# Reassociated linear attention with a critical-path scheduler, in a kernel of four interleaved layers

## The chip, the cores and the metric

The kernel runs on one core of one Trainium2 chip. The metric is the device time of one execution in microseconds (us). Engines are named as in the profile: PE (TensorE matmul), PEld (its weight loads), DVE (VectorE), ACT (ScalarE), POOL (GpSimd), SP (SyncE, which here only issues transfers). A difference is taken from the ratio to the kernel before in the same rounds.

## The reference

Two pairs of layers, each an attention layer A and a feed-forward layer B, on x of 2048 x 512, all residual, LayerNorm before each layer. Cut to what matters:

```python
def A(x, wqkv, wo):                       # x is the LayerNorm of the stream, 2048 x 512
    q, k, v = split_heads(x @ wqkv)       # 32 heads of 16
    phi = lambda t: jnp.where(t > 0, t + 1, jnp.exp(t)) + 1e-6
    pq, pk = phi(q), phi(k)
    kv  = einsum("bhsd,bhse->bhde", pk, v)
    z   = einsum("bhsd->bhd", pk)
    num = einsum("bhqd,bhde->bhqe", pq, kv)
    den = einsum("bhqd,bhd->bhq", pq, z)[..., None] + 1e-6
    return merge_heads(num / den) @ wo
def B(x, w1, w2):                         # 512 -> 1376 -> 512
    return maximum(x @ w1, 0) @ w2
```

kv and z are sums over all 2048 rows. Nothing of the second half of an attention layer can start before its last row has gone through the first half. I call that point the barrier, and what comes before it the first phase. The second attention layer's first phase is interleaved with the feed-forward layer before it; the first attention layer's is not, since nothing is there to interleave with.

## The kernel before

The kernel is a graph of operations. A list scheduler, run when the kernel is built, gives each engine a fixed order from a table of assumed durations; every engine then executes its list strictly in that order, waiting on semaphores. 128 rows are a tile, 4 tiles a chunk, 4 chunks the sequence. The parts that matter (cut):

```python
# first phase, tile i: k and v projection, phi(k) to SBUF, v to SBUF, then the sum over rows
mm_group([(ps[b],  Tb[i, c], wqkv[c, D:2*D]) for c in range(4)])      # 4 x 512 columns
phi_evac(b, pk_tile(i))            # 2 ACT passes over PSUM, DVE min/add (emscr), DVE max
mm_group([(ps[b2], Tb[i, c], wqkv[c, 2*D:3*D]) for c in range(4)])    # 4 x 512 columns
evac(vext[i], ps[b2])              # ACT or DVE; column 128 of each block of vext is 1
mm_group([(kv_region(j), pk_tile(i)[j], vext[i, j, 0:129]) for j in range(4)])  # kv and z
...
# second half, chunk t, tile i
mm_group([(den, pq[j, t][il], Zh[j]) for il in range(4) for j in range(4)])  # 16 x 8 columns
DVE: dene = den + 1e-6 ; rden = reciprocal(dene)                              # rows x heads
mm_group([(num[j], pq[j, t][il], KVbd[j]) for j in range(4)])         # 4 x 128 columns
DVE: xn[i] = num * rden            # then 4 PE transposes (or a transposing DMA) back to Tb
mm_group([(ps[b], Tb[i, c], wo[c]) for c in range(4)])                # 4 x 512 columns
resid(i)                           # DVE adds the residual; ACT squares it for LayerNorm
```

```python
def _list_schedule(ops, ...):      # before
    ...
    for e in ENGINES:              # look at the next WINDOW[e] operations in program order
        ...                        # take the one that can start first; ties go to program order
```

The full text is here:

## Time and profile before

The median was 308.69 us before the prediction, over three runs from 308.55 to 308.80 us.

| what | before | where it is read |
|---|---|---|
| PE busy share of the span | 96% | busy row of the page |
| chain of waits, PE share | 81% | page, part 4 |
| matmul step, 512 columns | 215.9 ns | timeline of PE |
| DVE, ACT busy in 28 us at the first barrier | 26.8, 21.3 us | windows view |

The two lines of the page, kernel before (busy us, share of the span, count of instructions; then the chain that ended last):

```profile
...
PE 295.0 (96%) x1729; PEld 147.5 (48%) x1755; DVE 174.7 (57%) x486; ACT 178.3 (58%) x359; POOL 18.8 (6%) x29
...
PE 81%; DVE 11%; ACT 4%; DMA 3%; issue 1%
...
```

PE is the engine that the time follows. A "busy" PE is not one at its peak, because the shown matmuls overlap, so I use steps from start to start. The timeline of PE, kernel before, over the dense stretch (start us, us, engine, line, operation, count):

```profile
...
87.97 9.66 PE L499 MATMUL ps<-Tb,w 128*128 128x512 bf16 x44
97.47 0.38 PE L499 MATMUL ps<-w,big 128*128 128x512 bf16 x1
```

44 matmuls start between 87.97 and 97.47 us, 215.9 ns each. The Trainium skill, "TensorE: Matmul & The Clock Gate", Part 1, gives 215.7 ns for a warm matmul of 512 columns (columns divided by 2.4 GHz plus 2.5 ns), and this trace agrees. With this step every matmul's cost can be summed, and what is left of a stretch is time that PE lost.

### The profile page before, as it was taken

Reading aid. Unit: us, or ns where it says so; the run is one execution under the profiler, and the core shown is the slowest. Engines: PE = TensorE matmul, PEld = TensorE weight load, DVE = VectorE, ACT = ScalarE, POOL = GpSimd, SP = SyncE. Lnnn points to the kernel's source line nnn. Section 1 sums busy time; section 2 is a strip of 40 time slices with the busy share of each in tenths; the row PEclk is TensorE's granted clock in tenths of the full one; section 3 lists DMA queues with packets and bytes.
Section 4 is the critical chain, followed back from the end, with each engine's and each line's share of the span. In section 5 each row is a group of like instructions: output and inputs, shape, how many; then the busy total and the mean of one; then the engine's idle time right before and its main releaser. Section 6 shows DMA issues by size and latency. Waiting matters only on the chain.

```text
span 307.2 us, 4498 instructions
## 1 busy us (share of the span) xinstructions
PE 295.0 (96%) x1729; PEld 147.5 (48%) x1755; DVE 174.7 (57%) x486; ACT 178.3 (58%) x359; POOL 18.8 (6%) x29
## 2 busy tenths in 40 slices
PE   8999999898999999999999999989889999999996
PEld 3455555565444444444544445556534444444444
DVE  5898867999830381384264556699994026030122
ACT  1897857777775385387673357767867605606100
POOL 3211000001200020010000110000111001000000
PEclk9999999999999999999999999999999999999999
DMA  7993400003550016030000033000266002302022
GB/s 229 358 329 70 69 2 0 2 0 67 109 102 0 0 29 109 1 67 3 0 1 2 9 60 68 2 0 2 41 115 121 2 0 68 68 2 68 0 68 70
DMA packets 41765, 17.79 MB, mean 58 GB/s; under 512 B 33584, under 2 KB 41232, under 8 KB 41744
## 3 DMA queue, kind: packets, MB, share of 16 engines
q1 hardware_dynamic: 41744, 17.50, 24.0%
q8 instruction: 14, 0.23, 0.3%
q14 instruction: 7, 0.06, 0.1%
HBM read 7.01 MB, written 2.10 MB: 30 GB/s over the span
## 4 chain that ended last, share of the span: by engine, by line
PE 81%; DVE 11%; ACT 4%; DMA 3%; issue 1%
PE ps L499 78%; DVE xn L612 5%; DMA Tb<-xn 3%; DVE xres L510 2%; PE ps L394 2%; ACT big L479 2%; ACT escr L481 2%; DVE rden L596 2%; DVE xn L444 1%; PE ps L465 1%; DVE big L485 1%; DVE dene L594 0%; DVE emscr L483 0%; ACT Tb L469 0%; DVE xin L652 0%
## 5 line engine op out<-in xcount | busy, mean ns | idle before, releaser
L499 PE MATMUL ps<-Tb,w 128*128 128x512 bf16 (+1 forms) x352 | 77.3, 379 | 1.9 <-DMA Tb<-xn 1.9
L499 PE MATMUL ps<-w,big 128*128 128x512 bf16 (+3 forms) x355 | 76.4, 373 | 0.4
L633 ACT ACTIVATE big<-ps 128x512 bf16<-128x512 f32 (+1 forms) x78 | 46.2, 595 | 29.2 <-PE ps L499 28.8
L499 PE MATMUL ps<-wqkv,Tb 128*128 128x512 bf16 x248 | 58.3, 379 | 1.1 <-ACT Tb L469 0.7
L499 PEld LDWEIGHTS ps<-Tb,w 128*128 128x128 bf16 (+1 forms) x352 | 35.0, 100 | 43.5 <-DMA Tb<-xn 2.9
L499 PEld LDWEIGHTS ps<-w,big 128*128 128x128 bf16 (+1 forms) x363 | 35.3, 97 | 40.6
L516 ACT ACTIVATE sqscr<-xres 128x512 bf16<-128x512 f32 x48 | 30.1, 630 | 41.8 <-DVE xres L510 40.8
L479 ACT ACTIVATE big<-ps 128x512 bf16<-128x512 f32 x64 | 39.2, 613 | 19.1 <-PE ps L499 19.0
L510 DVE SCALAR_TENSOR_TENSOR xres<-ps,xres 128x512 f32<-128x512 f32 x32 | 21.7, 686 | 38.6 <-PE ps L499 38.4
L481 ACT ACTIVATE escr<-ps 128x512 bf16<-128x512 f32 x64 | 39.3, 616 | 0.0
L507 DVE TENSOR_TENSOR xin<-ps,xres 128x512 bf16<-128x512 f32 x15 | 10.4, 692 | 48.8 <-PE ps L499 48.8
L499 PEld LDWEIGHTS ps<-wqkv,Tb 128*128 128x128 bf16 x256 | 24.2, 97 | 26.6 <-ACT Tb L469 0.9
L499 PE MATMUL ps<-wo,Tb 128*128 128x512 bf16 x118 | 28.1, 379 | 2.4 <-ACT Tb L469 1.9
L432 POOL TENSOR_TENSOR rstd<-veps,nhalf 128x4 f32<-128x4 f32 x15 | 15.6, 1041 | 236.6 <-DVE veps L430 218.8
L499 PE MATMUL ps<-Tb,wqkv 128*128 128x512 bf16 x128 | 29.2, 379 | 0.0
L485 DVE TENSOR_TENSOR big<-big,emscr 128x512 bf16<-128x512 bf16 x64 | 26.6, 419 | 1.3
L529 DVE CAST vext<-ps 128x512 bf16<-128x512 f32 x23 | 15.9, 691 | 18.5 <-PE ps L499 18.4
L469 ACT ACTIVATE Tb<-ps 128x512 bf16<-128x512 bf16 x29 | 16.3, 600 | 16.7 <-PE ps L465 16.6
L483 DVE TENSOR_SCALAR emscr<-escr 128x512 bf16<-128x512 bf16 x64 | 18.1, 285 | 5.3 <-ACT escr L481 5.1
L612 DVE TENSOR_TENSOR xn<-ps,rden 128x512 bf16<-128x512 f32 x32 | 20.2, 680 | 0.0
L499 PEld LDWEIGHTS ps<-wo,Tb 128*128 128x128 bf16 x128 | 11.9, 98 | 14.6 <-ACT Tb L469 1.7
L499 PEld LDWEIGHTS ps<-Tb,wqkv 128*128 128x128 bf16 x128 | 12.1, 97 | 12.8
(57 smaller groups left out, 190.0 us busy)
## 6 DMA issues: line engine op xcount, KB each, us to landing
wqkv<-in_A_wqkv_dram SPq DMA_DIRECT2D x3, 512.0 KB, 5.9
xin<-in_A_x_dram SPq DMA_DIRECT2D x3, 512.0 KB, 8.7
out_dram<-xin SPq DMA_DIRECT2D x3, 512.0 KB, 2.9
w<-in_B_w_dram SPq DMA_DIRECT2D x1, 1376.0 KB, 11.0
w<-in_B_w_dram SPq DMA_DIRECT2D x1, 1280.0 KB, 13.8
wo<-in_A_wo_dram SPq DMA_DIRECT2D x1, 512.0 KB, 8.8
xin<-in_A_x_dram SPq DMA_DIRECT2D x1, 384.0 KB, 3.2
Tb<-xn SPq DMA_TRANSPOSE x16, 4.3
```

Of the source, the lines that this page charges most:

```text
L432: g.add(POOL, lambda e: e.tensor_tensor(rstd[:, sl], veps[:, sl], nhalf[:, 0:4], ALU.pow), [("veps", t), ("nhalf",)], [("rstd", t)], C_POO ...
L469: g.add_flex([(ACT, lambda e: e.activation(dst, psb()[:, :], ACTF.Identity), C_ACT_PSUM), (DVE, lambda e: e.tensor_copy(dst, psb()[:, :]), ...
L479: g.add(ACT, lambda e: e.activation(dst_ap, psv[:, b, :], ACTF.Identity, bias=1.0 + 1e-6, scale=1.0), [("ps", b)], [dst_key], C_ACT_PSUM, ...
L481: g.add(ACT, lambda e: e.activation(escr[:, s, :], psv[:, b, :], ACTF.Exp), [("ps", b)], [("escr", s)], C_ACT_EXP, name=name + "_exp")
L483: g.add(DVE, lambda e: e.tensor_scalar(emscr[:, s, :], escr[:, s, :], 1.0, 1e-6, ALU.min, ALU.add), [("escr", s)], [("emscr", s)], C_DVE_B ...
L485: g.add(DVE, lambda e: e.tensor_tensor(dst_ap, dst_ap, emscr[:, s, :], ALU.max), [dst_key, ("emscr", s)], [dst_key], 340.0, name=name + "_ ...
L499: last = e.matmul(o, l, r, start=st, stop=sp, skip_group_check=skip)
L510: g.add(DVE, lambda e: e.scalar_tensor_tensor(xres[:, i, :], psv[:, b, :], 0.0, src, ALU.add, ALU.add, accum_out=s1[:, i:i + 1]), [("ps", ...
L516: g.add(ACT, lambda e: e.activation(sqscr[:, q, :], xres[:, i, :], ACTF.Square, accum_out=s2[:, i:i + 1]), [("xres", i)], [("sqscr", q), ( ...
L529: (DVE, lambda e: e.tensor_copy(vext[:, i, :, 0:128], psv[:, b2, :].rearrange("p (j f) -> p j f", f=128)), C_DVE_FLEX)],
L612: g.add(DVE, lambda e: e.tensor_tensor(xn[:, i, :].rearrange("p (h f) -> p h f", f=16), psv[:, b, :].rearrange("p (h f) -> p h f", f=16), ...
L633: g.add_flex([(ACT, lambda e, M=M, b=b, u=u: e.activation(unit_ap(u, M), psv[0:M, b, :], ACTF.Relu), C_ACT_PSUM), (DVE, lambda e, M=M, b=b ...
```

## The change

The intent was to give PE less work. Since v = x wv, the sum of pk by v over the rows is (sum of pk by x) times wv. So the v projection and its eviction go, and the sum G = x^T pk is accumulated instead in four PSUM banks. kv is multiplied into wo once (Wp), and q is scaled by 1/den in the transposed layout in which it is produced, so that the products num, their transposes and 1/den in row layout go. z is summed by POOL. 1/den is exp(-ln(den)) on ACT, because den is now spread over 128 partitions. The scheduler is replaced as well: among the operations that can start now, it takes the one with the longest path to the end. The diff, cut to its core:

```diff
+        if i == 0: POOL: zacc = pk_tile(0)
+        else:      POOL: zacc = zacc + pk_tile(i)            # 128 x 512, f32 + bf16
-        v projection, eviction to vext, kv accumulation 4 x 129 columns
+    def a_g_acc(i, GB):      # 4 x 512 columns into 4 PSUM banks
+        mm_group([(ps[GB[c]], xn[i, c], pk_tile(i)) for c in range(4)])
...
+    def a_z_final():         # zhi, zlo: zacc in two bf16 halves; 8 matmuls with ones; Zbd = mask * z
+    def a_kv():              # KVT = mask * (wv^T G), 16 x 128 columns
+    def a_wp():              # Wp[j] = KVT[j]^T wo[j], 4 x 512 columns, 4 evictions
...
     def a_den(t):
-        16 matmuls of 8 columns; dene; reciprocal
+        for j in range(4):
+            mm_group([(ps[b], Zbd[j], pq[j, t])])            # 1 x 512 columns
+            ACT: lden = Ln(ps[b] + 1e-6)
+            ACT: lden = Exp(-lden)
+            DVE: pq[j, t] = pq[j, t] * lden
-    def a_num(i): ...        # num, xn = num * rden, transposes
     def a_wo(i):
-        mm_group([(ps[b], Tb[i, c], wo[c]) for c in range(4)])
+        mm_group([(ps[b], pq[j, t][il], Wp[j]) for j in range(4)])
...
 def _list_schedule(ops, ...):
+    succ = _prioritise(ops)  # longest path from each operation to the end
-    # earliest start within a window of program order
+    st0 = min(c[0] for c in cands)
+    st, o = min((c for c in cands if c[0] <= st0 + SLACK[e]), key=lambda c: (-c[1].prio, c[1].idx))
```

The full diff also preloads a table of functions on ACT.

## The prediction

> **What bounds it now.** TensorE. The page's busy row gives PE 96%; the chain of waits is PE for 81% of the span. The timeline of PE shows 44 FFN matmuls of 512 columns starting over 87.97 to 97.47 us, 215.9 ns each (the Trainium skill, "TensorE: Matmul & The Clock Gate", Part 1, gives 215.7 warm; the trace agrees). Issue steps from the timeline: 216 ns (512 columns), about 57 (128), 26 (the 8-column den). Sum before: 1216 x 216 = 262.3; kv accumulation 128 x 58 = 7.5; num 7.2; transposes 7.2; den 3.3; warm-up 6.6: 294 us of the 307.2 us span. The remaining 13 us: start 1.2, first transpose eviction 0.9, tail 2.7, and the two attention barriers, 55.5-77.6 and 202.3-224.8, each 18.3 us of PE work in 22 us: 3.8 and 4.2 lost. The rest is dense.
>
> **What the change does to PE, per attention layer.** Removes v projection (64 x 216), kv accumulation, num, den, 48 transposes: 25.4 us. Adds the x-pk accumulation (64 x 216 = 13.8), transposed den (16 x 216 = 3.5), wo folding (0.9), kvT and z (24 small, 1.3): 19.5 us. Net -5.9 per layer, -11.8 in all. PE sum 282 us.
>
> **Other engines.** Per layer, ACT and DVE together lose 16 v evictions, 12 Tb evictions, 4 reciprocals (0.95), and 16 xn multiplies (replaced by u multiplies of about the same 0.6-0.7). ACT gains 16 Ln + 16 Exp of 0.5-0.6 us (as the exp evictions): 17 us, all after z is known. At the barrier ACT has late phi 7.9 + Ln/Exp 17 + squares 10 = 35 us against some 22-26 us of PE work: the last chunks' den is ACT-bound, but FFN matmuls of chunk 0 (9.5 us each of h and out) should cover them once its transpose DMA (4.3 us) lands. New chain at the barrier: G eviction, kvT, mask, wo folding, eviction, 6-7 us, and z sum to Zbd, Ln, Exp, u, 9-10 us before the first wo; late q (6.9 us), kvT and den fill part. I put the hole at 3 to 5 us per barrier, as now: O transposes leave the chain, ACT's Ln/Exp comes in.
>
> **Contention.** 16 POOL adds of 128x512 per layer, taken as 1.25 us (the change's own constant). The Trainium skill, "SBUF — State Buffer", "Who interferes with whom", says two-SBUF-input and 2-port DVE instructions block while POOL holds the shared ports. No trace here shows it yet. In layer 0's first phase (10-50 us; DVE busy 34 us in the windows view, about 26 without v casts) 19 us of POOL adds could stretch phi and delay G: I allow 2 us. G also holds 4 PSUM banks instead of 2: 0-1 us.
>
> **Sum.** 308.7 - 11.8 + 2 (contention, banks) - 1 to +1 (barriers, scheduler): 298; with credit for the scheduler 297 us, range 290.5 to 303.5. Chances: faster 0.84, within 2% 0.13, slower 0.03.
>
> **What would show each step.** Matmul count: 1256 of 512 columns, no vext or KVbd, 32 transposes. PE idle in the two barriers: 3-5 us each, released by ACT (Ln/Exp) or DVE u. ACT near full for 20 us after each barrier. POOL adds about 1.2 us; DVE phi max/emscr rise above 419/285 ns in layer 0.
>
> **What would make it wrong.** POOL adds slower than 1.25 us, or DVE blocked so z or phi lags several us (303+). ACT not covered by FFN work, holes of 7-10 us. Barriers filled (289-291).

## More of the kernel before

The windows view, kernel before, of 28 us at the first barrier and 22 us at the second (each engine's busy us and count, PEclk, DMA share, GB/s):

```profile
...
50.00:78.00 28.00, 24.96 (x253) 15.25 (x254) 26.80 (x76) 21.27 (x49) 1.94 (x2) 1.00 0.11 20
203.00:225.00 22.00, 18.50 (x204) 11.87 (x205) 21.96 (x59) 14.72 (x35) 2.01 (x2) 1.00 0.18 26
...
```

Here PE has work for most of the time, but DVE is busy for 26.80 of 28 us and 21.96 of 22 us: at the barriers DVE, not PE, is full.

The start of DVE's list, kernel before (in brackets: idle time before the instruction and what ended it):

```profile
...
2.89 0.69 DVE L412 BATCH_NORM_STATS2 bst<-xin 128x6 f32<-128x512 bf16 x1 [1.71 <-DMA xin<-in_A_x_dram]
...
6.32 0.14 DVE L696 SCALAR_TENSOR_TENSOR nbias<-mv,rstd 128x1 f32<-128x1 f32 x1
...
6.54 0.38 DVE L698 TENSOR_SCALAR xn<-xin,rstd,nbias 128x512 bf16<-128x512 bf16 x1
...
```

The statistics of the first tile begin at 2.89 us, its nbias follows at 6.32 and its normalisation at 6.54 us. PE's first real work, a transpose, starts at 7.67 us, right behind its warm-up matmuls.

The DVE instructions that will meet POOL, kernel before, groups view of 8 to 60 us (x count, busy us, mean ns of one, idle us before them):

```profile
...
L485 DVE TENSOR_TENSOR big<-big,emscr 128x512 bf16<-128x512 bf16 x32 | 13.2, 416 | 0.5
...
L483 DVE TENSOR_SCALAR emscr<-escr 128x512 bf16<-128x512 bf16 x32 | 8.9, 282 | 0.9 <-ACT escr L481 0.7
...
L444 DVE TENSOR_SCALAR xn<-xin,rstd,nbias 128x512 bf16<-128x512 bf16 x13 | 4.6, 405 | 0.1
...
```

## The result, and the profile after

The changed kernel takes 319.45 us (median of four runs, 318.89 to 320.67), the kernel before 308.62 us: slower, ratio 1.0359 (95% interval 1.0338 to 1.0380). Here and below a ratio is one kernel's to the other's in the same rounds, so it is not quite the ratio of the medians. Differences "by ratio" below are differences of such ratios times 308.6 us.

The page's two lines, kernel after:

```profile
...
PE 290.7 (91%) x1363; PEld 131.2 (41%) x1363; DVE 185.1 (58%) x461; ACT 192.9 (61%) x388; POOL 58.9 (19%) x60
...
PE 69%; ACT 14%; DVE 9%; DMA 5%; issue 2%; SPq 0%; DVEq 0%
...
```

PE's share fell to 91%, and ACT and DVE entered the chain. I summed the matmuls of each stage at columns / 2.4 GHz + 2.5 ns, but at no less than 26 ns, the step of the 8-column matmuls in the timeline of before, and took the rest as lost. The trace of after has all 1363 matmuls; that of before lacks 26 of 1755 (5.6 us). Its 1755 weight loads are all there, so the stage of each missing matmul is known. The figures here, and those of the same kind below, are corrected for it:

| us lost by PE (span less matmul work) | before | after |
|---|---|---|
| first phase, to the last accumulating matmul | 5.3 | 16.6 |
| first barrier, to the first FFN matmul | 3.8 | 8.1 |
| FFN with the second first phase | 0.3 | 1.4 |
| second barrier | 4.2 | 8.4 |
| rest | 2.9 | 4.3 |
| all | 16.5 | 38.8 |
| matmul work | 290.7 | 279.0 |

The work fell by 11.7 us, as intended. The lost time rose by 22.3 us, and the difference is the 10.6 us that the span grew. The timeline of PE, kernel after, rows with a hole ahead of them:

```profile
...
1.24 4.93 PE L402 MATMUL ps<-wrm 128*128 128x512 bf16 x16 [1.24 <-DVE wrm L395]
11.39 1.77 PE L470 MATMUL ps<-ident,xn 128*128 128x128 bf16 x12 [5.21 <-ACT xn L697]
12.95 5.05 PE L504 MATMUL ps<-wqkv,Tb 128*128 128x512 bf16 x12
...
46.00 2.76 PE L504 MATMUL ps<-wqkv,Tb 128*128 128x512 bf16 x12 [3.09 <-DMA Tb<-xn]
...
81.43 3.59 PE L504 MATMUL ps<-Wp,big 128*128 128x512 bf16 x8 [4.72 <-DVE big L609]
...
233.22 5.86 PE L504 MATMUL ps<-Tb,w 128*128 128x512 bf16 x20 [3.48 <-DMA Tb<-xn]
...
```

There are three kinds of hole. PE waits 5.21 us at the start, and the 12 matmuls from 12.95 us then take 4.88 us, about 407 ns each instead of 216: the clock had gone down (PEclk 0.66 of full speed in the mean from 10 to 20 us). The same page of the skill says that an idle window of about 3.4 us halves the clock; the trace agrees here, and again after the 4.72 us hole, where 8 matmuls take from 81.43 to 84.82 us, 424 ns each. So 1.7 of the 8.1 us of the first barrier are slow matmuls and not waiting. After the 3.48 us hole the next 20 matmuls take 285 ns each, which puts 1.4 us more under "rest"; after the 3.09 us hole the clock is full (217 ns each). In the first phase PE waits 3.09 us for a transposing DMA. At the barriers it waits for DVE's multiply (L609) and for a DMA.

The start of DVE's list, kernel after, to be read against that of before:

```profile
...
6.83 0.17 DVE L704 TENSOR_SCALAR veps<-mv 128x3 f32<-128x3 f32 x1
9.14 1.29 DVE L417 BATCH_NORM_STATS2 bst<-xin 128x6 f32<-128x512 bf16 x2 [2.14 <-DMA xin<-in_A_x_dram]
10.34 0.14 DVE L693 SCALAR_TENSOR_TENSOR nbias<-mv,rstd 128x1 f32<-128x1 f32 x1
10.40 0.69 DVE L417 BATCH_NORM_STATS2 bst<-xin 128x6 f32<-128x512 bf16 x1
...
```

and POOL's at the same time:

```profile
...
6.79 0.58 POOL L691 TENSOR_TENSOR rstd<-veps,nhalf 128x1 f32<-128x1 f32 x1 [4.54 <-DVE mv L418]
...
```

The first tile's 1/std was ready on POOL at about 7.4 us. The nbias that needs it comes at 10.34 us, because two statistics of the second chunk (L417 at 9.14 us) stand ahead of it in DVE's list, and these waited for their load until 9.14 us. An engine takes its list strictly in order, so a load that lands later than the scheduler assumed holds back work that was ready.

The DVE groups of 8 to 60 us, kernel after, and the POOL adds:

```profile
...
L532 POOL TENSOR_TENSOR zacc<-zacc,big 128x512 f32<-128x512 f32 x15 | 20.5, 1370 | 14.8 <-DVE big L490 10.3 <-DVE veps L425 3.7 <-DVE nbias L439 0.6
...
L486 ACT ACTIVATE escr<-ps 128x512 bf16<-128x512 f32 x26 | 16.2, 631 | 11.9 <-PE ps L504 6.0 <-DVE emscr L488 5.9
...
L490 DVE TENSOR_TENSOR big<-big,emscr 128x512 bf16<-128x512 bf16 x25 | 13.9, 573 | 1.0 <-ACT big L484 0.5
...
L488 DVE TENSOR_SCALAR emscr<-escr 128x512 bf16<-128x512 bf16 x26 | 9.4, 380 | 1.3 <-ACT escr L486 1.0
...
L449 DVE TENSOR_SCALAR xn<-xin,rstd,nbias 128x512 bf16<-128x512 bf16 x13 | 7.5, 610 | 0.0
...
```

The mean of the phi maximum rose from 416 to 573 ns, emscr from 282 to 380, the normalisation from 405 to 610. Single instructions show why. DVE and POOL, kernel after:

```profile
...
22.22 1.36 DVE L449 TENSOR_SCALAR xn<-xin,rstd,nbias 128x512 bf16<-128x512 bf16 x1
```

```profile
...
22.27 1.15 POOL L532 TENSOR_TENSOR zacc<-zacc,big 128x512 f32<-128x512 f32 x1
...
33.38 3.70 POOL L532 TENSOR_TENSOR zacc<-zacc,big 128x512 f32<-128x512 f32 x1 [3.73 <-DVE veps L425]
37.04 1.01 POOL L437 TENSOR_TENSOR rstd<-veps,nhalf 128x4 f32<-128x4 f32 x1
```

The normalisation at 22.22 us took 1.36 us instead of 0.40 and ended when the POOL add of 22.27 us had ended. At 33.38 us it is the other way round: an add took 3.70 us beside an unbroken row of DVE instructions, phi maxima and emscr in turn, that ended at 36.06 us, and LayerNorm's power (L437), behind it in POOL's list, started only at 37.04 us.

The windows view of the barriers, kernel after:

```profile
...
56.00:85.00 29.00, 23.76 (x116) 9.92 (x115) 25.30 (x66) 28.20 (x60) 2.58 (x2) 0.90 0.10 19
203.00:233.00 30.00, 22.82 (x119) 10.12 (x115) 25.37 (x72) 29.77 (x67) 2.80 (x3) 0.99 0.15 19
...
```

ACT is busy for 28.20 of 29 us and 29.77 of 30 us; DVE is at 25.3 in both. ACT took on the load, and DVE was hardly relieved.

### The profile page after: what moved, and what is told of

Read it like the earlier page. It is cut to its first block, busy times and chain, and to the rows that moved or that the text cites. A ratio compares the mean times of both kernels' runs of the same rounds, so it can differ in the third digit from the quotient of the medians.

```text
span 317.8 us, 3874 instructions
## 1 busy us (share of the span) xinstructions
PE 290.7 (91%) x1363; PEld 131.2 (41%) x1363; DVE 185.1 (58%) x461; ACT 192.9 (61%) x388; POOL 58.9 (19%) x60
## 4 chain that ended last, share of the span: by engine, by line
PE 69%; ACT 14%; DVE 9%; DMA 5%; issue 2%; SPq 0%; DVEq 0%
PE ps L504 68%; ACT lden L607 3%; ACT lden L605 3%; DMA Tb<-xn 3%; DVE xn L449 3%; ACT sqscr L521 3%; ACT escr L486 2%; DMA xin<-in_A_x_dram 2%; ACT big L484 2%; DVE big L490 2%; DVE bst L417 2%; DVE emscr L488 1%; ACT xn L447 1%; PE ps L470 0%; DVE nbias L439 0%
## 5 line engine op out<-in xcount | busy, mean ns | idle before, releaser
L504 PE MATMUL ps<-w,big 128*128 128x512 bf16 (+2 forms) x363 | 77.3, 372 | 0.0
L486 ACT ACTIVATE escr<-ps 128x512 bf16<-128x512 f32 x64 | 38.8, 627 | 18.5 <-PE ps L504 10.1
L532 POOL TENSOR_TENSOR zacc<-zacc,big 128x512 f32<-128x512 f32 x30 | 38.5, 1283 | 35.9 <-DVE big L490 31.3
L437 POOL TENSOR_TENSOR rstd<-veps,nhalf 128x4 f32<-128x4 f32 x15 | 16.1, 1078 | 150.9 <-DVE veps L435 146.2
L504 PE MATMUL ps<-Wp,big 128*128 128x512 bf16 x128 | 31.4, 395 | 8.0 <-DVE big L609 6.6
L504 PE MATMUL ps<-wqkv,Tb 128*128 128x512 bf16 x128 | 33.3, 401 | 5.1 <-DMA Tb<-xn 3.1
L490 DVE TENSOR_TENSOR big<-big,emscr 128x512 bf16<-128x512 bf16 x64 | 34.7, 560 | 3.2 <-ACT big L484 2.1
L504 PE MATMUL ps<-big,xn 128*128 128x512 bf16 x128 | 30.1, 379 | 0.0
L488 DVE TENSOR_SCALAR emscr<-escr 128x512 bf16<-128x512 bf16 x64 | 21.4, 346 | 14.7 <-ACT escr L486 13.4
L504 PEld LDWEIGHTS ps<-Wp,big 128*128 128x128 bf16 x128 | 12.4, 100 | 25.3 <-DVE big L609 7.8
L504 PEld LDWEIGHTS ps<-wqkv,Tb 128*128 128x128 bf16 x128 | 12.7, 103 | 22.2 <-DMA Tb<-xn 3.6
L609 DVE TENSOR_TENSOR big<-big,lden 128x512 bf16<-128x512 bf16 x32 | 20.7, 685 | 1.3 <-ACT lden L607 1.2
L605 ACT ACTIVATE lden<-ps,eps 128x512 f32<-128x512 f32 x32 | 20.2, 718 | 1.1 <-PE ps L504 1.1
```

Source lines behind the costliest of these rows:

```text
L437: g.add(POOL, lambda e: e.tensor_tensor(rstd[:, sl], veps[:, sl], nhalf[:, 0:4], ALU.pow), [("veps", t), ("nhalf",)], [("rstd", t)], C_POO ...
L486: g.add(ACT, lambda e: e.activation(escr[:, s, :], psv[:, b, :], ACTF.Exp), [("ps", b)], [("escr", s)], C_ACT_EXP, name=name + "_exp")
L488: g.add(DVE, lambda e: e.tensor_scalar(emscr[:, s, :], escr[:, s, :], 1.0, 1e-6, ALU.min, ALU.add), [("escr", s)], [("emscr", s)], C_DVE_B ...
L490: g.add(DVE, lambda e: e.tensor_tensor(dst_ap, dst_ap, emscr[:, s, :], ALU.max), [dst_key, ("emscr", s)], [dst_key], 340.0, name=name + "_ ...
L504: last = e.matmul(o, l, r, start=st, stop=sp, skip_group_check=skip)
L532: g.add(POOL, lambda e: e.tensor_tensor(zacc[:, :], zacc[:, :], pk_tile(i), ALU.add), [("big", pk_unit(i)), ("zacc",)], [("zacc",)], C_POO ...
```

## The experiments

Two theories at the start. Theory M: the new arithmetic costs it, by POOL adds that block DVE and by Ln and Exp on ACT at the barrier. Theory S: the new scheduler's order costs it.

| run | us, median | ratio to before (95%) | output |
|---|---|---|---|
| after | 319.45 | 1.0359 (1.0338 to 1.0380) | |
| e1 new arithmetic, old scheduler | 320.07 | 1.0362 (1.0317 to 1.0406) | correct |
| e2 old arithmetic, new scheduler | 328.22 | 1.0637 (1.0577 to 1.0696) | correct |
| e3 after, loads in program order | 314.11 | 1.0196 (1.0159 to 1.0233) | correct |
| e4 after, POOL adds on 8 columns | 312.41 | 1.0137 (1.0100 to 1.0174) | wrong |
| e5 after, Exp on 8 columns | 317.29 | 1.0276 (1.0255 to 1.0298) | wrong |
| e6 e3, e4 and e5 together | 306.27 | 0.9924 (0.9876 to 0.9973) | wrong |
| e7 e3 and z on PE | 310.14 | 1.0060 (1.0032 to 1.0089) | correct |
| e8 e2, loads in program order | 315.35 | 1.0212 (1.0190 to 1.0235) | correct |
| e9 e7, Exp and u on 8 columns | 301.42 | 0.9753 (0.9707 to 0.9799) | wrong |
| e10 e7, 1/den in bf16 | 307.02 | 0.9943 (0.9911 to 0.9975) | correct |
| e11 e7, den on 32 partitions | 310.97 | 1.0048 (0.9992 to 1.0104) | correct |
| e12 after, POOL memsets for the adds | 318.27 | 1.0302 (1.0278 to 1.0325) | wrong |

The "8 columns" runs and e12 keep the scheduler's table of durations, so the order of the instructions is exactly that of their base kernel; the traces show the same order on all engines. Only the length of the named instructions differs, and in e12 their kind. A stage figure is of the one profiled execution of a kernel, a ratio of all.

### e1: the new arithmetic under the old scheduler

```diff
-def _prioritise(ops): ... ; def _list_schedule(...): ...   # new
+def _list_schedule(...): ...                               # that of before
```

> The new arithmetic, put in order by the old scheduler (its window, its strict choice of engine). Theory S (the new scheduler's static order is what costs the time: loads out of order at the start, DVE held behind a late load, POOL adds ahead of the LayerNorm power): most of the loss goes, 295 to 303 us. Theory M (the new arithmetic itself costs it: POOL adds that block DVE, Ln and Exp on ACT at the barrier): 312 us or more, whatever the order.

Measured: 320.07 us. Theory M holds for the arithmetic: with the old scheduler it is just as slow. The loss only sits elsewhere. PE starts at 7.30 us and the first phase loses 9.6 us instead of 16.6, but the barriers lose 8.8 and 10.8 us instead of 8.1 and 8.4, and the stretch between them 4.6 instead of 1.4.

### e2: the old arithmetic under the new scheduler

```diff
-def _list_schedule(...): ...                               # that of before
+def _prioritise(ops): ... ; def _list_schedule(...): ...   # new
```

> The old arithmetic, put in order by the new scheduler. Theory S: slower than the kernel before, 313 to 320 us, and the first layer's start is late as in the changed kernel. Theory M: 304 to 310 us.

Measured: 328.22 us, which is more than theory S gave. So both theories hold, each for its half, and the parts do not simply add up: the scheduler costs the old arithmetic 20 us by ratio and the new arithmetic nothing. The timeline of PE, e2, shows where most of it is:

```profile
...
21.63 1.89 PE L469 MATMUL ps<-ident,xn 128*128 128x128 bf16 x16 [14.54 <-DVE xn L448]
...
```

PE stands for 14.54 us at the start. The transfers of this run, SP's timeline, show the reason: the 128 KB first tile of x (L365), from which everything starts, was put behind four transfers of x and two of w, at 9.07 us instead of 0.80.

```profile
...
2.92 6.10 SPq L363 DMA_DIRECT2D xin<-in_A_x_dram  x2
9.07 1.93 SPq L365 DMA_DIRECT2D xin<-in_A_x_dram  x1
...
```

### e3: the loads in program order

```diff
-st, o = min((c for c in cands if c[0] <= lim), key=lambda c: (-c[1].prio, c[1].idx))
+st, o = min((c for c in cands if c[0] <= lim), key=lambda c: (-c[1].prio if e != SP else 0.0, c[1].idx))
```

> The changed kernel, but the SyncE queue takes its ready transfers in program order (first x tile, rest of its chunk, wk, ...), all else by priority. Wrongly ordered loads as a cause: first transpose back from 11.4 to about 7.7 us, no cold clock at 10 to 20 us, about 5 to 6 us less, 313 to 315 us. Rival: the first phase is bound by DVE and POOL after the start anyway, so the gain is absorbed before the barrier: 317 us or more.

Measured: 314.11 us, 5.0 us less than after by ratio. PE, e3, at the start:

```profile
...
7.00 0.40 PE L470 MATMUL ps<-ident,xn 128*128 128x128 bf16 x4 [0.77 <-DVE xn L695]
8.09 1.04 PE L504 MATMUL ps<-wqkv,Tb 128*128 128x512 bf16 x4 [0.69 <-ACT Tb L474]
...
```

The first transpose is at 7.00 us, PEclk is at full speed from 10 to 20 us. The order of the loads, and DVE's list that was planned on it, cost 5 us of the changed kernel. (The edit puts all of SP's transfers in program order, the transposing ones too.) Beside e1 it shows something else: with the loads in order, the new scheduler is about 5 us better for the new arithmetic than the old one (1.0196 against 1.0362). Its order of the compute gave what its order of the loads took.

### e4: short POOL adds

```diff
-tensor_tensor(zacc[:, :],   zacc[:, :],   pk_tile(i),         ALU.add)
+tensor_tensor(zacc[:, 0:8], zacc[:, 0:8], pk_tile(i)[:, 0:8], ALU.add)
```

> The changed kernel with the same order of instructions on each engine, but each POOL add works on 8 of 512 columns (wrong result on purpose)[...]. Contention as a cause: the DVE phi maximum falls from 560 to about 420 ns, the 3.1 us hole before 46 us goes, 312 to 315 us. Rival, the adds run beside DVE at no cost: within 1 us of 319.

Measured: 312.41 us, 6.9 us less by ratio. The groups of 8 to 60 us, e4:

```profile
...
L490 DVE TENSOR_TENSOR big<-big,emscr 128x512 bf16<-128x512 bf16 x26 | 10.5, 420 | 1.5 <-ACT big L484 1.4
...
L488 DVE TENSOR_SCALAR emscr<-escr 128x512 bf16<-128x512 bf16 x27 | 7.6, 290 | 6.3 <-ACT escr L486 6.0
...
L532 POOL TENSOR_TENSOR zacc<-zacc,big 128x8 f32<-128x8 f32 x15 | 5.3, 356 | 21.6 <-DVE big L490 15.4 <-DVE veps L425 5.2 <-DVE nbias L439 0.7
...
L449 DVE TENSOR_SCALAR xn<-xin,rstd,nbias 128x512 bf16<-128x512 bf16 x13 | 4.7, 404 | 0.0
...
```

DVE's three kinds of instruction are back at 420, 290 and 404 ns; together they took 22.8 us against 30.8 in the changed kernel. The hole before 46 us is gone. In the traces the whole gain lies in the first phase, which loses 9.9 us instead of 16.6, while the barriers stay at 8.1 and 8.5. The order on all engines is the same, so the length of the POOL adds is what differs. Not all of the gain need be theirs, though. PE in e4, the same 12 matmuls that took from 12.95 to 17.83 us in the changed kernel:

```profile
...
13.16 3.44 PE L504 MATMUL ps<-wqkv,Tb 128*128 128x512 bf16 x12
16.45 0.39 PE L470 MATMUL ps<-ident,xn 128*128 128x128 bf16 x4
...
```

They took 3.29 us instead of 4.88, before any POOL add had run: the clock came back earlier in this execution, by chance as far as the record shows. So the adds cost between 5.3 us (an estimate, 6.9 less 1.6) and 6.9 us.

### e12: POOL as long busy, but writing only

```diff
-tensor_tensor(zacc[:, :], zacc[:, :], pk_tile(i), ALU.add)
+memset(zscr[:, :], 0.0)                                # 128 x 1300 f32
```

> The changed kernel, same order of instructions, each POOL add replaced by a POOL memset of 1300 f32 columns, an estimated 1.1 to 1.2 us from the 128x128 memsets (wrong result on purpose): POOL is as long busy, but reads nothing from SBUF. If the 7 us of the adds are POOL's queue (LayerNorm's power behind an add): 317 to 320 us. If they are the shared read ports: two-input DVE instructions no longer wait (phi maximum mean back to about 420 ns) and the time falls to 312 to 315 us; one-input DVE instructions may still be stretched.

Measured: 318.27 us, only 1.8 us less by ratio. The groups, e12:

```profile
...
L532 POOL MEMSET zscr<- 128x1300 f32 x15 | 17.9, 1197 | 15.9 <-DVE big L490 15.0 <-DVE nbias L439 0.6
...
L486 ACT ACTIVATE escr<-ps 128x512 bf16<-128x512 f32 x26 | 15.8, 610 | 10.3 <-DVE emscr L488 5.2 <-PE ps L504 5.0
...
L488 DVE TENSOR_SCALAR emscr<-escr 128x512 bf16<-128x512 bf16 x26 | 15.3, 605 | 2.0 <-ACT escr L486 1.8
...
L490 DVE TENSOR_TENSOR big<-big,emscr 128x512 bf16<-128x512 bf16 x26 | 10.4, 417 | 1.0 <-ACT big L484 0.4
...
L449 DVE TENSOR_SCALAR xn<-xin,rstd,nbias 128x512 bf16<-128x512 bf16 x13 | 7.5, 617 | 0.0
...
```

Neither of my two readings was right as it stood. The two-input phi maximum does run freely again at 417 ns, as the reading by ports said, but the one-input emscr went to 605 ns and the normalisation stayed at 617, so DVE's three kinds take 33.2 us, no less than before. The Trainium skill, "SBUF — State Buffer", "Who interferes with whom", says just this: a DVE instruction with two SBUF inputs contends only with a POOL instruction that reads SBUF, a one-input instruction in a two-port mode with any. The trace agrees on both halves (that emscr and the normalisation run in such a mode, it does not show). What counts is that POOL is long busy at all while DVE runs such instructions. The queue can play only a small part: without the 3.70 us add, LayerNorm's power starts at 33.68 instead of 37.04 us and the hole before the DMA is 1.34 instead of 3.09 us. POOL and PE, e12:

```profile
...
33.68 1.04 POOL L437 TENSOR_TENSOR rstd<-veps,nhalf 128x4 f32<-128x4 f32 x1
...
44.06 2.76 PE L504 MATMUL ps<-wqkv,Tb 128*128 128x512 bf16 x12 [1.34 <-DMA Tb<-xn]
...
```

### e5: short Exp

```diff
-activation(lden[:, s, :],   lden[:, s, :],   ACTF.Exp, scale=-1.0)
+activation(lden[:, s, 0:8], lden[:, s, 0:8], ACTF.Exp, scale=-1.0)
```

> The changed kernel with the same order of instructions on each engine, but each Exp behind the Ln works on 8 of 512 columns (wrong result on purpose). The full Exp takes about 0.52 us of ACT per piece, the short one an estimated 0.2, so about 5 us of ACT less at each barrier. ACT's Ln and Exp as the cause of the barrier holes: the 4.7 us hole and the 1.3 + 1.9 + 3.5 us ones shrink to about half or less, 311 to 314 us. Rival, the holes come from the length of the chain G, kvT, wo folding and the transposing DMA: 317 us or more.

Measured: 317.29 us, 2.6 us less by ratio; the short Exp took 224 ns in the mean instead of 678. This spoke for the rival, that the holes are the latency of the chain. e9 corrected that: DVE was busy for 18.8 of the 20 us from 60 to 80 us in this run, so it could take over as the limit.

### e6: the three together

> Loads in program order, POOL adds on 8 columns and Exp on 8 columns together (wrong result on purpose). If the three costs stand side by side, they add up: 319.5 - 5.3 - 7.1 - (what the short Exp gave), so 300 to 302 us. If the first two give back the same slack of the first phase: 304 to 308 us.

Edit: those of e3, e4 and e5. Measured: 306.27 us. By ratio the three take away 13.4 us, against 5.0 + 6.9 + 2.6 = 14.5 us one by one. That is in the range that I had given to the rival, that the first two give back the same slack, and the traces bear it out in part: in the first phase e3 saves 6.3 us, e4 6.7, and the two together 9.1 (16.6 to 7.5). So the costs of the loads and of the adds overlap; over the whole kernel the difference of 1.1 us is within the noise (1.5 us).

### e7: ordered loads and z on PE, a correct kernel

```diff
-POOL: zacc = zacc + pk_tile(i) ; zhi, zlo, 8 matmuls with ones
+mm_group([(ps[zb][:, j], pk_tile(i)[j], ones[:, 0:1]) for i in range(16) for j in range(4)])  # end of phase
```

> A correct version of the first two: loads in program order, and z summed by 64 one-column matmuls into one PSUM bank at the end of the first phase (about 26 ns each as the 8-column den before, 1.7 us of PE per layer, and the eight zb matmuls go) in place of the POOL adds. If the POOL adds were the cost by their hold on the ports: 319.5 - 5.3 - 7.1 + 2 = about 309, 306 to 311 us. If the order of DVE work around them was the cost: 312 us or more.

Measured: 310.14 us, inside the expected 306 to 311. By ratio it is 9.2 us better than after; e3 and e4 gave 11.9, but they overlap (e6), and the 64 small matmuls per layer cost some of it. The kernel is now within 1% of the one before, though PE has about 9 us less to do. What remains is the barriers: 6.8 and 7.5 us lost in the profiled execution, the fastest of five (307.46 us).

### e8: the old arithmetic, new scheduler, ordered loads

> The old arithmetic with the new scheduler, but loads in program order. If the 20 us that the new scheduler cost the old arithmetic are its load order (PE idle 14.5 us at the start, then half clock): 309 to 313 us. If its choice of order elsewhere costs as much: 318 us or more.

Edit: that of e3, on e2. Measured: 315.35 us, between the two. By ratio, 13.1 us of the 19.7 us that the new scheduler cost the old arithmetic were the loads. The cause of the other 6.5 us stays open: the first phase, the first barrier and the end lose 2.0, 2.3 and 1.5 us more than in the kernel before, and I did not take them apart.

### e9: Exp and the multiply both short

```diff
 # e7 and
-tensor_tensor(pq, pq, lden, ALU.mult)
+tensor_tensor(pq[:, 0:8], pq[:, 0:8], lden[:, 0:8], ALU.mult)     # and Exp as in e5
```

> The version with ordered loads and z on PE, with Exp and the multiply u both on 8 of 512 columns (wrong result on purpose); same order of instructions. Short Exp alone had given 2 us. If the barrier is bound by ACT and DVE together (ACT 100%, DVE 84 to 97% busy there), taking about 5 us of ACT and 8 us of DVE per barrier closes most of the holes: 299 to 303 us against 310. If the holes are the latency of the chain and of the transposing DMA: 306 us or more.

Measured: 301.42 us, 9.5 us below e7 by ratio. The barriers lose 2.6 and 3.6 us instead of 6.8 and 7.5. PE at the longest hole of the first barrier, e7 and then e9:

```profile
...
71.80 4.11 PE L501 MATMUL ps<-Wp,big 128*128 128x512 bf16 x12 [3.71 <-DVE big L600]
...
```

```profile
...
69.39 2.76 PE L501 MATMUL ps<-Wp,big 128*128 128x512 bf16 x12 [1.75 <-DVE big L600]
...
```

The shorter hole also leaves the clock alone: the 12 matmuls behind it take 2.73 us instead of 3.95. The chain has the same number of links and the same DMA in both. One pass through it is shorter by an estimated 1.0 us (the means of Exp and multiply fell from 702 and 685 to 231 and 161 ns), against about 4 us less lost at each barrier, so its latency was not the main cause: at the barrier ACT and DVE together have too much to do, and relieving ACT alone (e5) gave only 2.6 us.

### e10: 1/den in bf16, a correct kernel

```diff
-ACT: lden = Exp(-lden)            # f32
+ACT: rdb  = Exp(-lden)            # bf16
-DVE: pq = pq * lden
+DVE: pq = pq * rdb
```

> The version with ordered loads and z on PE, but Exp writes 1/den in bf16, so that the multiply u has two bf16 operands (0.42 us as the phi maximum takes, not 0.69). About 4 us of DVE less per barrier, ACT as before. If DVE shares the bound: 305 to 308 us. If ACT alone binds the barrier: 309 to 311 us.

Measured: 307.02 us, correct. By ratio 3.6 us below e7 and 0.6% below the kernel before (interval 0.9911 to 0.9975): the only correct kernel here that beats both, by little. The barriers lose 5.4 and 6.1 us. That fits DVE sharing the bound, but the edit also lowered the multiply's duration in the scheduler's table, and the traces show another order on ACT and DVE than in e7, so the gain is not shown to be the multiply's alone.

### e11: den on 32 partitions

```diff
-for j: den[128 x 512] ; Ln ; Exp ; multiply
+den[32 x 512] by 4 matmuls ; one Ln ; one Exp (bf16)
+for j: ps = hexp[j]^T rdc          # spread over 128 partitions, 512 columns
+       multiply by ps
```

> The version with ordered loads and z on PE, but den is made for 32 heads on 32 partitions, one Ln and one Exp for each chunk instead of four of each (about 13 us of ACT less per barrier), and 1/den is spread over the partitions by 16 more matmuls of 512 columns per layer (3.5 us of PE). If ACT's Ln and Exp are the binding part of the barrier: 301 to 306 us in spite of 7 us more PE work. If DVE or the chain binds: 309 to 316 us.

Measured: 310.97 us, not told apart from e7 or from the kernel before. It is not a sign against ACT: the barriers lose 3.9 and 5.0 us, together 5.4 less than in e7, but the 32 added matmuls are 6.9 us of PE. The relief was bought at its price.

## Why the prediction was wrong, point by point

**What bounded the kernel: right but incomplete.** PE work with two holes at the barriers was the account, and it closed: 3.8 and 4.2 us, as the table has them. I did not see that DVE was already the fuller engine there, with 26.80 busy us of 28; that it made the holes of before, no run tests.

**"Net -5.9 per layer, -11.8 in all": right.** Measured 290.7 - 279.0 = 11.7 us. The count of 1256 matmuls of 512 columns was right too (1245, and 22 of 256 columns).

**"I allow 2 us" for contention: the mechanism was right, the size was not.** It is 5.3 to 6.9 us (e4). I had estimated 19 us of POOL adds beside about 26 us of DVE work in 40 us, which was right (20.5 us from 8 to 60 us), and then took the waits as mostly hidden. They add 8.0 us to DVE's three kinds of instruction, and every tile's phi and every chunk's normalisation pass through them. POOL's own list was not weighed: the power of LayerNorm stands behind the adds.

**"With credit for the scheduler": there was none.** Under the old scheduler the new arithmetic takes as long (e1 1.0362, after 1.0359). The new order of the loads cost 5.0 us (e3), with a cold clock on top of the wait, and that ate up what the new order of the compute gave. I read the scheduler's diff for its compute order and did not ask what a longest-path rule does to loads, nor what DVE's list does if one lands late.

**"I put the hole at 3 to 5 us per barrier, as now": this is the largest error.** Measured 8.1 and 8.4 us, against 3.8 and 4.2 before. I had the sum that says so, 35 us of ACT against 22 to 26 us of PE, (Ln and Exp, put there at 17 us per layer, kept ACT busy for 19.3: 20.2 and 18.4 us over two layers in the groups view), and set it aside because "FFN matmuls of chunk 0 ... should cover them". They cannot cover before they exist: in the changed kernel chunk 0's transposing DMA was issued at 77.37 us, 21 us after the last accumulating matmul, since its statistics and its normalisation wait in the same full lists of ACT and DVE. e9 shows that this work is the cause: with less of it, 9.5 us go.

**The sum.** From the table, -11.7 (PE work) + 11.3 (first phase) + 4.3 and 4.2 (barriers) + 1.1 and 1.4 (FFN and rest) = 10.6, which is the measured growth of the span. Of the 11.3, taking away the loads' order and the adds together returns 9.1 (e6); the other 2.2 were not taken apart. Of the last 2.5, about 1.9 are matmuls at a lower clock behind the barriers' holes (0.5 and 1.4 us).

**Of the signs named beforehand,** the matmul count, the ACT load after each barrier, POOL adds of about 1.2 us (mean 1283 ns) and stretched DVE instructions all came; holes of 3 to 5 us did not. "What would make it wrong" named two of the three causes, and gave them too little weight.

## What to carry to other kernels

When a change moves work off the bounding engine, sum the busy time of the other engines in each stage, not over the whole span: a stage where one of them is already full pays for everything added there, and work of a later stage covers nothing until its inputs have passed through that same stage. A fixed order of instructions is only as good as the assumed landing times of its loads, so keep the first loads in the order of first use and check what stands behind each one. An idle engine that shares ports with a busy one is not free capacity.

## What the Trainium skill lacked or had wrong

- "SBUF — State Buffer", "Who interferes with whom": its rule was confirmed in both halves (e12: two-input DVE 417 ns, one-input 605 ns beside a writing POOL). It gives no size for a mixed stream. Here 15 POOL adds (20.5 us in all) stretched DVE by 8.0 us in 52 us and cost 5.3 to 6.9 us of the time, and one add took 3.70 us beside a row of DVE instructions.
- "GPSIMD Engine Reference", section 3.1, gives the two-input add for 2048 columns only (4497 ns), beside a rate of about 2.6 cycles per element. Here 512 columns (f32 and bf16 to f32) take 1.15 to 1.28 us in most cases, 8 columns 0.20 us at the least, and a memset of 1300 f32 columns, for which it has no figure, 1.18 us in most cases.
- No page that I used warns of a fixed in-order list behind a late load; here it cost 5.0 us, clock included. The halved clock after an idle stretch is in "TensorE: Matmul & The Clock Gate", Part 1, and was seen: about 407 ns for each of 12 matmuls after a wait of 5.21 us.
